# A gate over twelve consecutive tokens, the conv folded into the key-value product, and key products moved to GpSimd

## The chip, the cores and the metric

The kernel runs on one core of a Trainium2 chip. The metric is the device time of one execution in microseconds (us): the median of 3 runs of the kernel before is 76.44 us (75.55 to 77.24). The profiled execution took 76.63 us; the trace of it spans 74.9 us, so the measured time is about 1.7 us longer than the span of the trace.

Five engines work side by side: TensorE (PE in the profile; its weight loads are PEld), VectorE (DVE), ScalarE (ACT), GpSimd (POOL) and SyncE (SP, which here only issues transfers). Each works through its own instructions in order.

## The reference

Two layers, one after the other. The first is a linear attention with a second-degree feature map, the second a causal depthwise convolution that gates a linear unit. There are 4 batches, 4 heads, 1088 tokens, 32 elements per head.

```python
def phi(x):                          # S1, S2: 8 x 32
    a = einsum('rd,bhsd->bhsr', S1, x)
    b = einsum('rd,bhsd->bhsr', S2, x)
    return einsum('bhsi,bhsj->bhsij', a, b).reshape(..., 64)

q_p, k_p = phi(q), phi(k)
kv  = einsum('bhsf,bhsd->bhfd', k_p, v)          # sum over all tokens of a batch
z   = sum(k_p, axis=2)
num = einsum('bhsf,bhfd->bhsd', q_p, kv)
den = einsum('bhsf,bhf->bhs', q_p, z)[..., None] + 1e-06
x   = num / den                                  # heads side by side: b, s, 128

xp = concatenate([zeros((B, 4, 128)), x], axis=1)
gate_pre = sum over k of conv_w[k] * xp[:, k:k + S, :]      # 5 taps
gate = 1 / (1 + exp(-gate_pre))
out  = (gate * (x @ w_val)) @ w_out
```

## The kernel before

A batch's 1088 tokens are 32 blocks `j` of 34 consecutive tokens `T`; the 34 `T` (padded to 36) are 3 *units* of 12, and a unit is 3 *chunks* of 128 columns, 4 `T` by 32 `j`. There are N = 12 units in all. A main loop of *steps* works on several units at once, each a few steps further on: the keys of unit i+1, the queries of unit i-2, the gate of unit i-6, the output of unit i-7.

For the keys: a 32x32 block transpose on DVE, the projections `abk` on PE (fp32), a copy to SBUF on ACT, the outer products (two chunks on DVE, one on POOL), and the sums `kv` and `z` on PE.

```python
def k_phi(i):
    ...
    outer(DVE, phik, ab[:, 0, :ND]..., ab_sb[:, 1], 0, ND * H)     # ND = 2 chunks of 3
    outer(POOL, phip, ab_sb[:, 0]..., ab_sb[:, 1], ND * H, H)      # the third chunk

def k_z(i):                       # z by matmul; each chunk's product with all three, 96 columns
    for t in range(NCK):
        PE.matmul(kv_ps[b][t * HR : (t + 1) * HR, R2:], lhsT=..., rhs=ab_sb[:, t * HR : (t + NCK) * HR], ...)
```

When the three units of a batch are summed, `kv` becomes weights. The value weights `kw` are `kv` times `w_val`; the gate weights `wg` are `kv`, transposed, times each of the five taps:

```python
def finish_c(b):                  # z times S2: the third part of rhsq
    PE.matmul(c_ps, lhsT=s2t, rhs=zm, ...); SCA.copy(out=rhsq[b][:, 2, :], in_=c_ps)
def finish_kvm(b):
    PE.transpose(kvm_ps, kvx, identf); SCA.copy(out=kvm, in_=kvm_ps)
def finish_wg(b, g):              # twice per batch
    POOL.tensor_mul(wg[b][:, g], kvm[:, g]..., cwrep[:, :, ...])   # cwrep: conv_w, one copy per partition
```

For the queries: transpose, projections with `z` folded in, normalise, outer product, transpose back into feature-major columns `phiT`.

```python
def q_ab(i):
    ...  # 12 fp32 matmuls abq<-rhsq,qT
    SCA.copy(out=ac, in_=ab[:, 0:3:2]...)
    POOL.tensor_mul(prod[:, :, 0:r], ac[:, 0], ac[:, 1])
def q_den(i):
    DVE.reduce_sum(den, prod); DVE.reciprocal(rden, den)
    POOL.tensor_mul(an, ac[:, 0], rden...)
def q_phi(i):
    DVE.tensor_mul(phiq, an..., ab[:, 1]...)          # 768 elements per partition
def q_pt(i):
    ...  # 6 PE transposes of phiq into pt
    for g in range(2):
        SCA.copy(out=phiT[b][:, g, HALO:]..., in_=pt[:, g]...)
    if u == U - 1:
        ...  # halo: two POOL copies of the last 4 T of all blocks, one block further
```

A block's first tokens need the last four `T` of the block in front of it for the convolution. That is the *halo*; since those `T` lie in the third unit, the gate of a batch's first unit waits for its third unit here.

The gate and the output:

```python
def g_mm(i):     # 10 matmuls (5 taps, 2 halves) of 384 columns, then 2 for the value
    ...
    SCA.activation(out=gate, in_=g_ps, func=ACT.Sigmoid)
def g_gv(i):     DVE.tensor_mul(gv, gate, v_ps)
def g_out(i):
    ...          # 3 matmuls o_ps<-w_out_sb,gv, 1 or 2 ACT copies to o_sb
    for m in range(M4):      # 4 transfers per unit, runs of one token (512 bytes)
        (SCA if i == N - 1 and m % 2 else nc.sync).dma_start(out=o_d[:, T0 + m : last : M4, :], in_=o_sb[J * m : J * (m + 1), :nc_, :])
```

Loads are all issued by SP at the start: k and v of batch 0, q of batch 0, then k, v and q of each later batch, with `cwrep` (conv_w copied to 128 partitions, 320 KB) in batch 1. PSUM: three shared buffers for `abk` and `abq`, three for gate, value and output, one each for `kv` and `pt`.

Of the kernel before, what the change touches and what calls it, by code (L numbers as in the profile page):

```python
# [16 lines left out]
def kernel(  # L17
# [19 lines left out]

    nc = tc.nc
# [3 lines left out]
    P = 128  # L42
# [7 lines left out]
    HALO = (KT - 1) * J  # L50
    eps = 1e-6

    const = ctx.enter_context(tc.tile_pool(name="const", bufs=1))
    work = ctx.enter_context(tc.tile_pool(name="work", bufs=3))
    ps_ab = ctx.enter_context(tc.tile_pool(name="ps_ab", bufs=3, space=bass.MemoryType.PSUM))
# [14 lines left out]
    PE, DVE, SCA, POOL = (Pinned(e) for e in (nc.tensor, nc.vector, nc.scalar, nc.gpsimd))  # L70
# [10 lines left out]
    phiT = [ctile([P, 2, HALO + U * W], BF16, f"phiT{b}") for b in range(B)]  # L81
# [7 lines left out]
    cwrep = ctile([P, KT, P], F32, "cwrep")  # L89
    warm = ctile([P, 1], F32, "warm")  # L90

    def kq_rows(src, b):
        return src[b].rearrange("h (j T) d -> (h j) (T d)", j=J)

    def load_all(src, dst, b):
        nc.sync.dma_start(out=dst[:, : NT * D], in_=kq_rows(src, b))

    def load_v(b):
        for h in range(H):
            head = v[b, h]  # L100
            dst = v_sb[b][:, h].rearrange("p T d -> p (T d)")

            def rows(j0, j1, m0, m1, n):
                nc.sync.dma_start(  # L104
                    out=dst[M4 * j0 + m0 : M4 * (j1 - 1) + m1, : n * D],
                    in_=bass.AP(
                        tensor=head.tensor, offset=head.offset + (NT * j0 + TM * m0) * D,
                        ap=[[NT * D, j1 - j0], [TM * D, m1 - m0], [1, n * D]],
                    ),
                )  # L110

            if b < B - 1 or h < H - 1:
                rows(0, J, 0, M4, TM)
            else:
                rows(0, J - 1, 0, M4, TM)
                rows(J - 1, J, 0, M4 - 1, TM)
                rows(J - 1, J, M4 - 1, M4, NT - TM * (M4 - 1))

    DVE.memset(v_sb[B - 1][3 * J :, H - 1, NT - 3 * TM :, :], 0.0)
    load_all(k, k_sb[0], 0)  # L120
    for x, Sx in enumerate((S1, S2)):
        SCA.dma_start(out=s_raw[x * r : (x + 1) * r], in_=Sx)
    load_v(0)
# [4 lines left out]
    for _ in range(7):  # L128
        PE.matmul(warm_ps, lhsT=zeros[:, :P], rhs=zeros, start=True, stop=True)

    DVE.memset(warm, 0.0)
# [8 lines left out]
    )  # L140
    hm = ctile([P, H], F32, "hm")
    DVE.memset(hm, 0.0)
    for h in range(H):
        DVE.memset(hm[h * D : (h + 1) * D, h : h + 1], 1.0)
    S3 = ctile([P, 2, HR], F32, "S3")

    def fill_k(b):
        POOL.memset(k_sb[b][:, NT * D :], 0.0)

    def fill_q(b):  # L150
        POOL.memset(q_sb[b][:, NT * D :], 0.0)
        POOL.memset(phiT[b][:, :, :HALO], 0.0)
        POOL.tensor_copy(out=rhsq[b][:, 0:2, :], in_=S3)

    fill_k(0)
# [6 lines left out]
    for _ in range(2):  # L162
        PE.matmul(warm_ps, lhsT=zeros[:, :P], rhs=zeros, start=True, stop=True)
# [7 lines left out]

    m2 = ctile([P, 2], F32, "m2")
# [9 lines left out]
    def early_constants():  # L182
        POOL.memset(mz4, 1.0)
        for sign, base in ((1, 0), (-1, r - 1)):
            POOL.affine_select(
                out=mz4, in_=mz4, pattern=[[-sign * D, H], [-sign * r, H]],
                compare_op=ALU.is_ge, fill=0.0, base=base, channel_multiplier=sign,
            )
        for h in range(H):
            POOL.memset(m2[h * D : (h + 1) * D, h % 2 : h % 2 + 1], 1.0)  # L190
            POOL.memset(m2[h * D : (h + 1) * D, 1 - h % 2 : 2 - h % 2], 0.0)
        for i in range(NPROD):
            POOL.memset(prods[i][:, :, r:], eps)

    def late_constants():
        DVE.reduce_sum(mz, mz4.rearrange("p x h -> p h x"), axis=AX.X)
        POOL.tensor_copy(out=s2x, in_=S3[:, 1].unsqueeze(1).to_broadcast([P, NCK, HR]))
        s2_ps = ps_g.tile([NCK * HR, P], F32, tag="g", name="s2_ps")
        PE.transpose(s2_ps, s2x.rearrange("p t x -> p (t x)"), identf)
        SCA.copy(out=s2t, in_=s2_ps)  # L200
        POOL.tensor_copy(out=identity, in_=identf)

    def load_weights():
        POOL.memset(w_val_sb, 0.0)
        for g in range(2):
            gs = slice(R2 * g, R2 * (g + 1))
            POOL.dma_start(out=w_val_sb[gs, g], in_=moe_w_val[gs])
        POOL.dma_start(out=w_out_sb, in_=moe_w_out)


    load_all(q, q_sb[0], 0)
    for b in range(1, B):
        load_all(k, k_sb[b], b)
        load_v(b)
        if b == 1:
            nc.sync.dma_start(out=cwrep, in_=moe_conv_w.unsqueeze(0).to_broadcast([P, KT, P]))
        load_all(q, q_sb[b], b)
# [4 lines left out]
    zab = {}  # L222
    abks, abss, phks, abqs, acs, prs, ans, pqs, vgs, gvs = ({} for _ in range(10))
# [5 lines left out]
    def block_transpose(src, dst, u, order):  # L229
        DVE.transpose(  # L230
            out=dst[:, u * W : (u + 1) * W].rearrange(f"p (t {order}) -> p t m j", t=NCK, m=M4),
            in_=src.rearrange("p (m u t d) -> p u t m d", m=M4, u=U, t=NCK)[:, u],
        )


    def k_T(i):
        b, u = divmod(i, U)
        block_transpose(k_sb[b], kT[b], u, "j m")

    def k_ab(i):  # L240
        b, u = divmod(i, U)
        ab = ps_ab.tile([P, 2, NCK, HR], F32, tag="ab", name="abk")
# [6 lines left out]
        ab_sb = work.tile([P, 2, NCK * HR], F32, tag="ab_sb", name="ab_sb")  # L249
        SCA.copy(out=ab_sb, in_=ab.rearrange("p x t c -> p x (t c)"))  # L250
        abks[i], abss[i] = ab, ab_sb
        zab[i] = ab_sb

    ND = NCK - 1

    def k_phi(i):
        ab, ab_sb = abks.pop(i), abss.pop(i)

        def outer(eng, dst, a, bb, lo, n):
            eng.tensor_mul(  # L260
                dst,
                a.unsqueeze(3).to_broadcast([P, n, r, r]),
                bb.rearrange("p (x j) -> p x j", j=r)[:, lo : lo + n]
                .unsqueeze(2)
                .to_broadcast([P, n, r, r]),
            )

        phik = work.tile([P, ND * H, r, r], F32, tag="phik", name="phik")
        phip = work.tile([P, H, r, r], F32, tag="phip", name="phip")
        outer(DVE, phik, ab[:, 0, :ND].rearrange("p t (h i) -> p (t h) i", h=H), ab_sb[:, 1], 0, ND * H)  # L270
        outer(
            POOL, phip, ab_sb[:, 0].rearrange("p (x i) -> p x i", i=r)[:, ND * H :], ab_sb[:, 1],
            ND * H, H,
        )
        phks[i] = phik, phip

    def k_kv(i):
        b, u = divmod(i, U)
        phik, phip = phks.pop(i)
        for t in range(NCK):  # L280
            for h in range(H):
                src = phik[:, t * H + h] if t < ND else phip[:, h]
# [4 lines left out]
                    start=(h == H - 1 and u == 0 and t == 0),  # L287
                    stop=(u == U - 1 and t == NCK - 1),
# [289 lines left out]
```

## Time and profile before

| what | before |
|---|---|
| time, median of 3 | 76.44 us |
| span of the profiled run | 74.9 us |
| PE busy, weight loads busy | 53.8 us, 37.2 us |
| DVE, ACT, POOL busy | 46.4, 33.9, 31.6 us |
| HBM read, written | 7.28 MB, 2.23 MB |
| share of the last chain: PE, DVE, DMA | 37%, 17%, 12% |

Busy times overlap, so none of them is a bound by itself. The kernel has stages: loads run at 308 to 399 GB/s until about 20 us, the main loop fills the middle, and after the last unit's products only PE, ACT and the output transfers are at work. In the views a line `L68` stands for the helper that issues nearly all instructions, so rows are told apart by the tiles: `phiq<-an,abq` is the product that writes `phiq`. A name without a number (`kT`) stands for all buffers of that name. Tile names such as `mz` and `S` are those of the kernel with their digits cut.

A useful clock for the loop is the start of the twelve `phiq` products on DVE, one per unit: 19.36, 22.94, 26.55, 30.63, 34.64, 38.29, 42.69, 46.35, 50.87, 55.32, 57.70 and 60.74 us.

### The profile page before, as it was taken

How to read it: one execution, taken by the hardware profiler on the slowest of the kernel's cores; microseconds unless marked ns; L12 is line 12 of the kernel's file. 1: busy time of each engine (PE TensorE's matmuls, PEld its weight loads, DVE VectorE, ACT ScalarE, POOL GpSimd, SP SyncE). 2: the span in 40 equal slices, each digit the busy share in tenths (PEclk: the TensorE clock that was granted, in tenths of full speed). 3: DMA queues.
4: the chain of work that ended last, by engine and by line, in shares of the span. 5: the costliest groups of instructions: out<-in, count | busy, mean ns of one | idle time of the engine just before them, and what ended most of it. 6: DMA issues, size and time to landing. Idle time of an engine off the chain costs nothing.

```text
span 74.9 us, 2969 instructions
## 1 busy us (share of the span) xinstructions
PE 53.8 (72%) x1215; PEld 37.2 (50%) x1215; DVE 46.4 (62%) x104; ACT 33.9 (45%) x95; POOL 31.6 (42%) x94
## 2 busy tenths in 40 slices
PE   2969950969667549979679992997996995995000
PEld 0313930859445427666566852864744664652000
DVE  3019965093797889797999699769089482232000
ACT  0700410123162626383825845566658687366100
POOL 5400698402426595617474654195262663000000
PEclk9999997555999999999999999999999999999755
DMA  0898899999965600000022040121313123332540
GB/s 5 281 305 132 308 363 371 368 339 372 399 219 143 227 24 27 0 0 17 0 53 61 0 113 5 41 55 27 79 26 79 25 58 86 103 85 67 142 112 18
DMA packets 9058, 9.62 MB, mean 128 GB/s; under 512 B 1493, under 2 KB 7893, under 8 KB 9045
## 3 DMA queue, kind: packets, MB, share of 16 engines
q1 hardware_dynamic: 8517, 9.29, 39.3%
q0 software_dynamic: 304, 0.07, 0.9%
q8 instruction: 9, 0.15, 0.8%
q10 hardware_dynamic: 224, 0.08, 0.4%
q14 instruction: 4, 0.03, 0.1%
HBM read 7.28 MB, written 2.23 MB: 127 GB/s over the span
## 4 chain that ended last, share of the span: by engine, by line
PE 37%; DVE 17%; DMA 12%; ACT 7%; SPq 6%; POOL 6%; issue 6%; ACTq 0%; POOLq 0%
PE g_ps L68 11%; DMA k_sb<-in_k_dram 10%; PE abq L68 7%; PE v_ps L68 4%; ACT phiT L68 4%; DVE kT L68 4%; DVE phiq L68 4%; PE kv L68 4%; DVE gv L68 3%; SPq L104 3%; PE abk L68 3%; PE pt L68 3%; PE o_ps L68 3%; DVE phik L68 2%; DMA out_dram<-o_sb 2%
## 5 line engine op out<-in xcount | busy, mean ns | idle before, releaser
L68 PE MATMUL g_ps<-phiT,wg 128*64 128x384 bf16 (+1 forms) x120 | 12.3, 321 | 1.0 <-POOL phiT L68 0.8
L68 DVE TENSOR_TENSOR phiq<-an,abq 128x768 bf16<-128x768 f32 x12 | 11.4, 951 | 2.6 <-POOL an L68 2.3
L68 PE MATMUL abk<-S,kT 128*32 128x64 f32 x288 | 7.8, 260 | 5.3 <-DVE kT L68 4.5
L68 ACT COPY phiT<-pt 128x384 bf16<-128x384 bf16 x24 | 10.3, 482 | 2.8 <-PE pt L68 2.6
L68 DVE STREAM_TRANSPOSE kT<-k_sb 128x384 f32<-128x384 f32 x12 | 10.0, 859 | 0.8 <-DMA k_sb<-in_k_dram 0.8
L68 POOL TENSOR_TENSOR phip<-ab_sb 128x256 f32<-128x256 f32 x12 | 7.5, 628 | 6.3 <-ACT ab_sb L68 6.3
L68 PE MATMUL abq<-rhsq,qT 128*32 128x96 f32 x288 | 9.3, 260 | 1.2 <-POOL rhsq L68 0.8
L68 PEld LDWEIGHTS abk<-S,kT 128*32 128x32 f32 x288 | 6.0, 133 | 7.7 <-DVE kT L68 3.8
L68 POOL TENSOR_TENSOR prod<-ac 128x96 f32<-128x96 f32 x12 | 4.7, 390 | 11.5 <-ACT ac L68 11.5
L68 DVE TENSOR_TENSOR gv<-gate,v_ps 128x384 bf16<-128x384 bf16 (+1 forms) x12 | 6.0, 502 | 4.8 <-PE o_ps L68 2.5
L68 POOL TENSOR_TENSOR an<-ac,rden 128x96 f32<-128x96 f32 x12 | 4.2, 352 | 10.5 <-DVE rden L68 8.3
L68 ACT COPY ab_sb<-abk 128x192 f32<-128x192 f32 x12 | 3.9, 323 | 10.4 <-PE abk L68 9.6
L68 PEld LDWEIGHTS <-wg 128*64 128x64 bf16 x120 | 6.6, 109 | 3.8 <-issue 1.3
L68 DVE TENSOR_TENSOR phik<-abk,ab_sb 128x512 f32<-128x512 f32 x12 | 8.2, 684 | 0.4 <-ACT ab_sb L68 0.4
L68 ACT ACTIVATE gate<-g_ps 128x384 bf16<-128x384 f32 (+1 forms) x12 | 5.7, 476 | 5.4 <-PE g_ps L68 5.3
L68 PE MATMUL kv<-phik,v_sb 128*32 128x64 f32 x192 | 7.5, 237 | 0.5 <-issue 0.5
L68 PEld LDWEIGHTS abq<-rhsq,qT 128*32 128x32 f32 x288 | 6.8, 116 | 2.1 <-POOL rhsq L68 0.9
L68 ACT COPY ac<-abq 128x192 f32<-128x192 f32 x12 | 3.9, 322 | 8.1 <-PE abq L68 7.3
L68 POOL TENSOR_TENSOR wg<-kvm,cwrep 128x320 bf16<-128x320 f32 x8 | 6.9, 866 | 0.3 <-ACT kvm L68 0.3
L68 DVE STREAM_TRANSPOSE qT<-q_sb 128x384 f32<-128x384 f32 x12 | 6.6, 549 | 0.6 <-DMA q_sb<-in_q_dram 0.6
L68 ACT COPY o_sb<-o_ps 128x384 f32<-128x384 f32 (+2 forms) x16 | 6.1, 404 | 1.9 <-PE o_ps L68 1.6
L68 PE MATMUL pt<-identity,phiq 128*128 128x128 bf16 x72 | 6.1, 220 | 0.7 <-DVE phiq L68 0.7
(60 smaller groups left out, 77.5 us busy)
## 6 DMA issues: line engine op xcount, KB each, us to landing
k_sb<-in_k_dram SPq DMA_DIRECT2D x4, 544.0 KB, 7.9
q_sb<-in_q_dram SPq DMA_DIRECT2D x4, 544.0 KB, 7.1
v_sb<-in_v_dram SPq DMA_DIRECT2D x15, 144.0 KB, 5.2
out_dram<-o_sb SPq DMA_DIRECT2D x39, 48.0 KB, 1.6
cwrep<-in_moe_conv_w_dram SPq DMA_DIRECT2D x1, 320.0 KB, 6.9
out_dram<-o_sb SPq DMA_DIRECT2D x7, 32.0 KB, 1.6
v_sb<-in_v_dram SPq DMA_DIRECT2D x1, 139.5 KB
out_dram<-o_sb ACTq DMA_DIRECT2D x1, 48.0 KB, 1.6
```

The lines of the kernel that those rows point to most:

```text
L68: return lambda *a, **k: tc.keep_in_program_order(call(*a, **k))
L104: nc.sync.dma_start(out=dst[M4 * j0 + m0 : M4 * (j1 - 1) + m1, : n * D], in_=bass.AP(tensor=head.tensor, offset=head.offset + (NT * j0 + T ...
```

## The change

The change rewrites where the work stands; the arithmetic is that of the reference as before. Its purposes: take work off DVE, start the loop earlier, let a batch's first gate not wait for its third unit, and store the output in fewer and longer runs.

- **Keys.** After the first three units all three chunks' outer products are made on POOL (`ND = 0`). The first three units still give DVE two chunks.
- **Queries.** A chunk now holds four `T` by 32 `j` token-major, so the transpose of q is a plain one over 384 contiguous columns, and `phiT` is written by one ACT copy of 768 elements. The units of a batch are taken in the order 2, 0, 1, so that the halo is ready first. The halo is one POOL copy.
- **Gate.** 12 consecutive `T`; `g_gv` writes its product reordered, so that an output partition holds three consecutive tokens: runs of 1.5 KB, one transfer per unit (two for a batch's last unit).
- **Conv weights.** `wg` no longer comes from a transpose and two POOL products: two fp32 matmuls multiply `kv` with a constant `dcw` (a diagonal per tap), and ACT copies them to bf16. `cwrep` goes; conv_w is loaded as 5 rows.
- **z** is 3 matmuls of 32 columns, `c` is 4 small matmuls.
- **Loads.** k and q of batches 2 and 3 are issued by POOL within the loop; the others by SP, in another order. The constants are set up earlier on POOL.
- **PSUM.** `abk` has one buffer of its own, shared with `c`, `kw` and half of `wg`; `abq` has two.
- The whole step has a new order.

```diff
-    ps_ab = ctx.enter_context(tc.tile_pool(name="ps_ab", bufs=3, space=bass.MemoryType.PSUM))
+    ps_k = ctx.enter_context(tc.tile_pool(name="ps_k", bufs=1, space=bass.MemoryType.PSUM))
+    ps_q = ctx.enter_context(tc.tile_pool(name="ps_q", bufs=2, space=bass.MemoryType.PSUM))
 ...
+    SP.dma_start(out=s_raw[:r], in_=S1)
+    SCA.dma_start(out=s_raw[r:], in_=S2)
+    load(k, k_sb, 0)
+    SCA.dma_start(out=cw_nat, in_=moe_conv_w)
+    load(q, q_sb, 0)
+    load(k, k_sb, 1)
     load_v(0)
+    load_v(1)
+    load(q, q_sb, 1)
+    load_v(2)
+    load_v(3)
 ...
+    def n_dve(i):
+        return 2 if i < U else ND                  # ND = 0
 ...
+    def finish_wg(b):
+        for g, (pool, tag) in enumerate(((ps_k, "k"), (ps_g, "g"))):
+            wg_ps = pool.tile([P, KT, 2 * D], F32, tag=tag, name="wg_ps")
+            PE.matmul(wg_ps, lhsT=fin["kvx"][gs], rhs=dcw[gs], start=True, stop=True)
+        for g in range(2):
+            SCA.copy(out=wg[b][:, g], in_=wps[g])
-        POOL.tensor_mul(wg[b][:, g], fin["kvm"][:, g]..., cwrep[:, :, ...])
 ...
+    QU = (2, 0, 1)
 ...
+            if i < N - 1:
+                SP.dma_start(out=rows, in_=src)
+            else:
+                for m in range(nm):
+                    (SCA if m % 2 else SP).dma_start(out=rows[m], in_=src[J * m : J * (m + 1)])
 ...
+    k_T(0); k_ab(0); k_cp(0); constants_1(); k_T(1); k_ab(1); k_cp(1); k_z(0); constants_2()
+    k_T(2); k_ab(2); k_cp(2); k_phiP(0, 2); k_z(1); q_T(0); k_z(2); k_phiD(0); finish_zm(0)
+    finish_c(0); k_phiP(1, 2); k_phiP(2, 2); k_phiD(1)
+    for s in range(2, N + 3):
+        ...                                         # at s == 2 also q_ab(0), k_T(3), q_T(1), k_phiD(2), load k of batch 2
+        k_ab(s + 1); k_cp(s + 1); q_ab(s - 2); q_cp(s - 2)
+        q_phi(s - 3); g_gv(s - 6); q_prod(s - 2); k_kv(s)
+        q_den(s - 2); k_phiP(s + 1, 2); q_an(s - 2); k_T(s + 2); q_T(s)
+        k_phiP(s + 1, 1); k_phiP(s + 1, 0)
+        q_pt(s - 3); q_ev(s - 3); q_halo(s - 3); g_val(s - 5)
+        g_out(s - 6); g_ev(s - 6); g_st(s - 6)
+        ...                                         # finish_kw, finish_wg, finish_c, finish_kv by step
+        g_mm(s - 5); g_sig(s - 5)
+        ...                                         # s == 2, 3, 4: load q2, k3, q3 on POOL
+    # after the loop: value, gate and output of the last two units
```

(Shortened: the calls of a step are written without their range checks, and setup code is left out.)

## The prediction

> **What bounds the kernel now.** I read the busy line first, then busy time by stage, one step of the loop on DVE and on PE, the costs of the POOL operations, and last the transfers at the end.
>
> ```profile
> PE 53.8 (72%) x1215; PEld 37.2 (50%) x1215; DVE 46.4 (62%) x104; ACT 33.9 (45%) x95; POOL 31.6 (42%) x94
> ```
>
> 72% for PE is an average over stages. The stage table (start:end, length, busy PE, PEld, DVE, ACT, POOL, granted clock, DMA share, GB/s) says more:
>
> ```profile
> 15.00:23.00 8.00, 5.49 (x150) 4.81 (x151) 5.78 (x14) 2.97 (x10) 2.26 (x7) 0.74 0.92 316
> 23.00:34.00 11.00, 8.41 (x293) 6.49 (x296) 9.88 (x21) 5.81 (x17) 6.33 (x16) 1.00 0.20 68
> 34.00:51.00 17.00, 14.21 (x379) 10.18 (x367) 14.48 (x32) 9.85 (x29) 10.03 (x24) 1.00 0.15 38
> 51.00:62.00 11.00, 10.16 (x156) 6.50 (x157) 7.43 (x16) 7.54 (x22) 4.99 (x14) 1.00 0.20 52
> 62.00:70.00 8.00, 5.64 (x56) 3.39 (x53) 2.08 (x4) 4.71 (x13) 0.58 (x2) 1.00 0.33 87
> ```
>
> To 23 us loads run (DMA 0.92) and nothing is full; from 23 to 51 DVE is busy 24.4 of 28 us and PE 22.6; later DVE drops out. One step in the timeline of DVE (start, length):
>
> ```profile
> 34.64 0.95 DVE L68 TENSOR_TENSOR phiq<-an,abq 128x768 bf16<-128x768 f32 x1 [0.48 <-POOL an L68]
> 35.51 0.68 DVE L68 TENSOR_TENSOR phik<-abk,ab_sb 128x512 f32<-128x512 f32 x1
> 36.11 0.85 DVE L68 STREAM_TRANSPOSE kT<-k_sb 128x384 f32<-128x384 f32 x1
> 36.81 0.54 DVE L68 STREAM_TRANSPOSE qT<-q_sb 128x384 f32<-128x384 f32 x1
> 37.27 0.22 DVE L68 TENSOR_REDUCE den<-prod 128x12 f32<-128x108 f32 x1
> 37.53 0.23 DVE L68 RECIPROCAL rden<-den 128x12 f32<-128x12 f32 x1
> 37.67 0.49 DVE L68 TENSOR_TENSOR gv<-gate,v_ps 128x384 bf16<-128x384 bf16 x1
> 38.13 0.19 DVE L68 TENSOR_TENSOR zm<-kv,mz 96x32 f32<-96x32 f32 x1
> 38.29 0.95 DVE L68 TENSOR_TENSOR phiq<-an,abq 128x768 bf16<-128x768 f32 x1
> ```
>
> Each starts where the last one leaves off: this step is 3.65 us of DVE with no gap. By start-to-start it is phiq 0.87, phik 0.60, kT 0.70, qT 0.46, den 0.26, rden 0.14, gv 0.46, zm 0.16. Between the phiq of 19.36 and of 50.87 us lie 8 steps, so a step takes 3.94 us: DVE's 3.65 or less plus a wait. PE is close behind:
>
> ```profile
> 46.66 0.54 PE L68 MATMUL abk<-S,kT 128*32 128x64 f32 x24
> ...
> 48.12 1.00 PE L68 MATMUL g_ps<-phiT,wg 128*64 128x384 bf16 x10
> 49.05 0.50 PE L68 MATMUL v_ps<-phiT,kw 128*128 128x384 bf16 x2
> 49.39 0.50 PE L68 MATMUL pt<-identity,phiq 128*128 128x128 bf16 x6
> 49.72 0.33 PE L68 MATMUL o_ps<-w_out_sb,gv 128*128 128x128 bf16 x3
> 49.98 0.28 PE L68 MATMUL kv<-ab_sb 128*32 128x96 f32 x3
> ```
>
> From 46.66 to 49.98 PE passes a whole step in 3.3 us: abk, z, kv and abq 1.46, gate 0.93, value 0.34, pt 0.33, out 0.26. POOL in the groups (busy, mean ns):
>
> ```profile
> L68 POOL TENSOR_TENSOR phip<-ab_sb 128x256 f32<-128x256 f32 x12 | 7.5, 628 | 6.3 <-ACT ab_sb L68 6.3
> ...
> L68 POOL DMA_DIRECT2D w_val_sb<-in_moe_w_val_dram x2 | 1.2, 610 | 0.3 <-POOL w_val_sb L68 0.3
> ```
>
> One chunk's product costs POOL 0.63 us where two cost DVE 0.68; a small transfer costs its issuer 0.61. The end, on SP's queue:
>
> ```profile
> 55.03 17.66 SPq L484 DMA_DIRECT2D out_dram<-o_sb  x30
> ```
>
> The last result is in SBUF at 69.58, but SP issues until 72.69: some 0.45 us per transfer with four per unit, a backlog. 1.6 us later (median landing) the last one lands; the span ends at 74.9.
>
> **What the Trainium skill says.** "GPSIMD Engine Reference", section 4.1 (Engine selection), puts two-input elementwise work on GpSimd at about half of VectorE's speed. The trace agrees for this form: 2.45 ns per element against 1.34. "FP8 and Floating Point Precision", section "TensorE Precision Notes", counts four passes through the array for true fp32; no row shows passes, and the trace has two matmul records per fp32 call (24 for 12). I use it for `wg`. "DMA: Bandwidth & Descriptors", section "Issuing engines are not separate DMA queues", says another issuing engine saves only the sequencer's time. The backlog above is just that time, so longer runs with fewer issues should show.
>
> **Part by part, in four stages.**
>
> *Start to the first phiq (19.36 now).* S1 and S2 come by two queues, an estimated 0.4 us sooner, so kT(0) starts near 5.4 (now 5.84). But DVE's second instruction is the reduction to `mz`, which waits for POOL, where the constants now stand first: memsets and mask 1.2, three weight transfers 1.8, identity 0.3, some ten small memsets 1.4, `id64` 0.3, `dcw` about 0.8 (320 elements at 2.45 ns), `mz4` 0.6 — from 0.8 to about 7.4 us, by the rows of before. So kT(1) starts near 7.6, later than now. Then kT(2), qT(0), phik(0) end near 10.2. abk(2) needs the PSUM buffer phik(0) reads, so it follows: +0.5 abk, 0.35 copy, 0.3 z, 0.2 zm, 0.4 c, 0.2 copy, and abq(0) runs near 12.3 to 13.0. Now it runs at 16.3, since a whole later unit and its load (k at 12.11) stood in front. DVE from zm on: phik 0.6, kT 0.7, qT 0.46, phik 0.6, den and rden 0.5, kT 0.7, qT 0.46, kvx 0.2, in all 4.2. First phiq near 16.3: 3.1 us gained.
>
> *Eleven steps to the last phiq (41.4 now, to 60.74).* DVE loses phik: 3.65 - 0.60 = 3.05, no bound any more. POOL has three phip at 0.66, prod 0.36, an 0.36: 2.7 per step, plus a halo of about 0.3 in three; the two wg (0.83 each) and the fills go. In the steps s = 2, 3, 4 it also issues a transfer of 544 KB, estimated at 0.8, and den waits behind that: I walked these to phiq at 16.3, 19.2, 23.0 and 26.5, two of the three near 3.6. PE: z is narrower (-0.05) and c and the transpose go (-0.35 per batch), while wg adds 320 columns x 4 passes / 2.4 per ns = 0.53 us per matmul by the skill's passes, 0.53 to 1.07 per batch. So 3.3 + 0.3 = 3.55 to 3.6 per full step: **PE becomes the bound**. ACT: ab_sb 0.32, ac 0.32, phiT about 0.8, o_sb 0.5, gate 0.5, plus a third of kvt, kw, wg and rhsq (1.8): 3.0. Five full steps at 3.65 make 18.25; the next has no abk (3.3), the last two neither abk nor kv (2.6 each). Sum 10.2 + 18.25 + 8.5 = 36.95, last phiq at 53.25: 4.4 us gained.
>
> *Last phiq to the last o_sb (8.84 now).* With the units in the order 2, 0, 1 the gate of the batch's first unit needs no halo of the last: the POOL copy (0.30) and the 0.82 us PE waits for it go. From phiq: 1.0 to pt, then PE 4.4 (pt 0.33, three values 1.0, gates 0.93 + 0.93 + 0.8, two outputs 0.4), gate 0.45, gv 0.5, output 0.5, copy 0.53, with small gaps 7.5: 1.3 gained, o_sb at 60.75.
>
> *Last o_sb to the end (5.3 now).* No backlog: one transfer for each earlier unit. The last unit's six go three on SP and three on ACT, 3 x 0.43 + 1.6 + 0.6 = 3.5: 1.8 gained.
>
> Span 64.2. The measured time lies 1.7 above the profiled span: 65.9. I add 0.6 for waits a sum of busy times leaves out: **66.5 us**.
>
> **Rivals.** (1) *POOL becomes the bound.* phip has no slack in the early steps, and a 544 KB transfer may cost the issuer more than 0.6 us. For it: prod, an and den form a loop through POOL, DVE and back. Against: 2.7 per step is under PE's 3.55. If POOL needed 3.7 per step, the time would be some 69. (2) *PSUM turns into waits.* abk has one buffer, shared with c, kw and wg; PE would wait for ACT once or more per step. At 0.4 per step it gives back 4 us: 70. (3) *Loads.* k2, q2, k3 and q3 start at about 12 us or later, beside v; if q1 or k2 comes late, early steps slip by up to 2 us: 68. The 544 KB transfers land in 7 to 8 us now, and k2 is wanted near 22, so I don't expect it. (4) *Better than thought:* wg's two matmuls use different rows of the array and may overlap, and PE may reach 3.4: 64.
>
> **Range and chances.** The stages gain 3.1, 4.4, 1.3 and 1.8; the last two rest on plain rows, the first two on walks that can be off by 2 us each, mostly to the slow side: 62.8 to 71. To lose the whole gain, two rivals would have to hold in full: faster 0.93, within 2% 0.04, slower 0.03.
>
> **What would show it right or wrong.** First phiq at 16 to 17 us; steps of 3.5 to 3.8 between the phiq of units 3 and 8 with PE over 90% busy there and DVE under 85%; no SP backlog and under 4 us after the last o_sb; no PE wait for the POOL halo. Wrong, if den, an or kv wait on POOL in late steps (rival 1), abk on ACT (2), or kT or qT on a load (3).

## The result and the profile after

The changed kernel takes 73.12 us (median, 72.50 to 73.63), the kernel before on the same chip 76.38 us. The ratio is 0.958 with a 95% interval of 0.945 to 0.971. On another chip, in a later set, the ratio was 0.971 (0.962 to 0.981). So the change makes the kernel faster by 3 to 4%, where 13% was predicted: the direction was right, the size was not, and 73.1 lies above the predicted range. (In most sets some runs were a few per cent longer than the rest; the ratios leave them out, the medians don't.)

The busy line of the kernel after, which answers to the first line shown of before:

```profile
PE 52.3 (73%) x1250; PEld 37.0 (52%) x1250; DVE 41.3 (58%) x107; ACT 35.6 (50%) x92; POOL 35.6 (50%) x94
```

DVE lost 5.1 us of work and POOL gained 4.0, as the change meant. The span fell only from 74.9 to 71.6 us. The stage table, in the same stretches as before (start:end, length, busy PE, PEld, DVE, ACT, POOL, granted clock, DMA share, GB/s):

```profile
15.00:23.00 8.00, 6.02 (x223) 4.75 (x211) 6.08 (x14) 4.08 (x10) 7.26 (x16) 1.00 0.70 231
23.00:34.00 11.00, 10.37 (x299) 7.72 (x299) 8.57 (x20) 7.30 (x18) 8.12 (x18) 1.00 0.27 87
34.00:51.00 17.00, 15.59 (x426) 11.81 (x424) 13.00 (x32) 11.85 (x32) 9.79 (x21) 1.00 0.19 52
51.00:62.00 11.00, 9.32 (x112) 5.67 (x111) 4.84 (x11) 6.89 (x17) 1.42 (x4) 1.00 0.22 63
62.00:70.00 8.00, 0.56 (x5) 0.22 (x3) 0.55 (x2) 1.25 (x4) 0.00 (x0) 0.63 0.34 70
```

From 23 to 51 us PE is now busy 26.0 of 28 us and DVE 21.6: the two have changed places. The last row is the surprise. From 62 us on almost nothing computes, yet the kernel runs for nearly 10 us more. Before, that stretch still held 5.64 us of PE.

The clock of the twelve `phiq` on DVE now reads 16.15, 19.39, 23.08, 27.00, 30.24, 34.34, 38.55, 41.75, 45.27, 49.05, 51.87 and 55.48 us; the last `o_sb` is written at 63.94. With these the span splits as the prediction split it:

| stage | before | predicted | after |
|---|---|---|---|
| start to first phiq | 19.36 | 16.3 | 16.15 |
| first to last phiq | 41.4 | 36.95 | 39.33 |
| last phiq to last o_sb | 8.84 | 7.5 | 8.46 |
| last o_sb to the end | 5.3 | 3.5 | 7.66 |
| span | 74.9 | 64.2 | 71.6 |

The last stage was to become shorter by 1.8 us and became longer by 2.4.

A step on DVE and the start of one on PE (start, length; in brackets the idle time before it and what ended it):

```profile
34.34 0.91 DVE L70 TENSOR_TENSOR phiq<-an,abq 128x768 bf16<-128x768 f32 x1
35.18 0.54 DVE L70 TENSOR_TENSOR gv<-gate,v_ps 128x256 bf16<-128x256 bf16 x2
36.79 0.27 DVE L70 TENSOR_REDUCE den<-prod 128x12 f32<-128x108 f32 x1 [1.07 <-POOL prod L70]
```
```profile
34.79 0.54 PE L70 MATMUL abk<-S,kT 128*32 128x64 f32 x24 [0.30 <-ACT rhsq L70]
35.15 0.68 PE L70 MATMUL abq<-rhsq,qT 128*32 128x96 f32 x24
```

DVE now has a hole of 1.07 us in a step that had none. PE has almost none; the one shown is a wait of 0.30 us for ACT. POOL makes all later `phip`, 30 in place of 12, each as long as before:

```profile
L70 POOL TENSOR_TENSOR phip<-ab_sb 128x256 f32<-128x256 f32 x30 | 18.4, 625 | 3.0 <-ACT ab_sb L70 3.0
L70 POOL TENSOR_TENSOR prod<-ac 128x96 f32<-128x96 f32 x12 | 4.6, 386 | 13.0 <-ACT ac L70 9.8 <-PE kv L70 3.2
```

POOL stands idle 13 us in front of `prod`, waiting for ACT and PE, so it is not the bound of the full steps. In the early steps it comes near to it: from 15 to 23 us it is busy 7.26 of 8 us, two issues of loads (0.59 us each) among that. The issues of output on SP, and the tail in stretches of 1 us, in the same columns as above:

```profile
29.78 36.30 SPq L70 DMA_DIRECT2D out_dram<-o_sb  x17
```
```profile
64.00:65.00 1.00, 0.00 (x0) 0.00 (x0) 0.00 (x0) 0.00 (x0) 0.00 (x0) 0.50 0.25 95
65.00:66.00 1.00, 0.00 (x0) 0.00 (x0) 0.00 (x0) 0.00 (x0) 0.00 (x0) 0.50 0.41 64
66.00:67.00 1.00, 0.00 (x0) 0.00 (x0) 0.00 (x0) 0.00 (x0) 0.00 (x0) 0.50 0.84 127
67.00:68.00 1.00, 0.00 (x0) 0.00 (x0) 0.00 (x0) 0.00 (x0) 0.00 (x0) 0.50 0.59 118
68.00:69.00 1.00, 0.00 (x0) 0.00 (x0) 0.00 (x0) 0.00 (x0) 0.00 (x0) 0.50 0.14 51
69.00:70.00 1.00, 0.00 (x0) 0.00 (x0) 0.00 (x0) 0.00 (x0) 0.00 (x0) 0.50 0.05 15
```

SP has 17 issues for the whole output where the kernel before has 46, and it issues the store of unit 10 at 62.75 us, as soon as that result is in SBUF. So the backlog of issues is indeed gone. Instead the transfers themselves are slow: while a unit is stored the 16 DMA engines are busy 0.25 on average and move some 95 GB/s. A share of 0.25 is what 4 engines of 16 would give. The new store has the pattern `m j (c e)` in DRAM, and its outermost dimension `m` has four entries.

The Trainium skill states this rule: "DMA: Bandwidth & Descriptors", section "Why a DMA increments its semaphore by 16 and not by 1", says that a transfer is spread over the largest number of engines, up to 16, that divides the size of the slowest dimension of both its patterns. Here the two sizes are 4 (`m`) and 128 (the partitions of `o_sb`), which gives 4, and the measured share of 0.25 agrees. The prediction cited that page for the cost of issuing and passed over this rule.

**Theory after the result.** (A) Most of the miss is the tail: stores on four engines, with the last unit's pieces behind the store of the unit before. (B) The drain adds to it: near the end PE waits for the last `phiq` (1.18 us) and for PSUM buffers. Rivals: (C) the tail is the issue and landing of the last unit's own six transfers; (D) DVE or POOL still sets the steps, and moving the outer products was worth little; (E) the shared PSUM buffer `ps_k` costs the steps.

### The profile page after: what moved, and what is told of

Read it like the earlier page. It is cut to its first block, busy times and chain, and to the rows that moved or that the text cites. A ratio compares the mean times of both kernels' runs of the same rounds, so it can differ in the third digit from the quotient of the medians.

```text
span 71.6 us, 2999 instructions
## 1 busy us (share of the span) xinstructions
PE 52.3 (73%) x1250; PEld 37.0 (52%) x1250; DVE 41.3 (58%) x107; ACT 35.6 (50%) x92; POOL 35.6 (50%) x94
## 4 chain that ended last, share of the span: by engine, by line
PE 41%; POOL 17%; DVE 12%; issue 10%; ACT 8%; POOLq 1%; ACTq 0%
PE abq L70 8%; PE abk L70 8%; PE g_ps L70 7%; PE kv L70 6%; POOL phip L70 5%; DVE kT L70 5%; POOL prod L70 4%; PE pt L70 3%; PE wg_ps L70 3%; ACT gate L70 3%; DVE phiq L70 3%; PE v_ps L70 2%; POOL w_val_sb L70 2%; DVE den L70 2%; PE o_ps L70 2%
## 5 line engine op out<-in xcount | busy, mean ns | idle before, releaser
L70 POOL TENSOR_TENSOR phip<-ab_sb 128x256 f32<-128x256 f32 x30 | 18.4, 625 | 3.0 <-ACT ab_sb L70 3.0
L70 ACT COPY phiT<-pt 128x768 bf16<-128x768 bf16 x12 | 9.6, 798 | 5.3 <-PE pt L70 5.3
L70 PE MATMUL g_ps<-phiT,wg 128*64 128x384 bf16 (+1 forms) x120 | 11.6, 320 | 0.3 <-ACT gate L70 0.2
L70 DVE TENSOR_TENSOR gv<-gate,v_ps 128x384 bf16<-128x384 bf16 (+2 forms) x16 | 6.6, 431 | 5.5 <-ACT gate L70 5.5
L70 PEld LDWEIGHTS <-wg 128*64 128x64 bf16 x120 | 7.1, 109 | 3.5 <-issue 2.7
L70 DVE TENSOR_REDUCE den<-prod 128x12 f32<-128x108 f32 x12 | 3.2, 266 | 6.7 <-POOL prod L70 6.7
L70 PE MATMUL kv<-phip,v_sb 128*32 128x64 f32 x240 | 6.1, 229 | 0.0
L70 PE MATMUL v_ps<-phiT,kw 128*128 128x384 bf16 (+1 forms) x24 | 5.7, 317 | 0.3 <-ACT gate L70 0.3
```

The source lines that it names most:

```text
L70: return lambda *a, **k: tc.keep_in_program_order(call(*a, **k))
```

## The experiments

The kernels below are the changed kernel with the edit shown, unless another base is named. "Tail" is from the end of the last `o_sb` to the end of the span.

| run | what | time, us (n) | ratio to before | tail, us |
|---|---|---|---|---|
| e1_jm | all units' stores with j outermost | 70.63 (4) | | 3.4 |
| e2_split | four transfers per unit | 71.22 (4) | 0.932 (0.922 to 0.942) | 5.6 |
| e3_two | two transfers per unit, m of 2 outermost | 80.22 (1) | | 9.85 |
| e7_jmtail | j outermost in the last two units only | 70.25 (4) | 0.927 (0.915 to 0.940) | 3.8 |
| e13_skip10 | store of unit 10 left out | 69.65 (6) | 0.918 (0.909 to 0.927) | 3.8 |
| e14_after | the changed kernel, beside e13, e15, e16 | 73.68 (6) | 0.971 (0.962 to 0.981) | 7.5 |
| e15_jmtail | e7 again, beside them | 69.85 (6) | 0.926 (0.920 to 0.932) | 3.8 |
| e4_nd2 | two of three key chunks on DVE | 79.94 (4) | 1.053 (1.042 to 1.063) | |
| e5_nd2_sbuf | the same, DVE reads SBUF | 76.62 (4) | 1.011 (1.002 to 1.021) | |
| e6_qu | units in the order 0, 1, 2 | 80.25 (4) | 1.042 (1.028 to 1.056) | |
| e8_tail_all | e7 + last abq earlier + free PSUM | 69.38 (4) | 0.913 (0.903 to 0.923) | 4.1 |
| e16_tail_all | e8 again | 69.65 (6) | 0.913 (0.903 to 0.924) | 3.9 |
| e9_wgbf | e7 + bf16 wg | 70.82 (4) | 0.928 (0.913 to 0.943) | |
| e10_kwpt | e7 + kw_ps in pt's buffer | 70.90 (4) | 0.943 (0.930 to 0.956) | |
| e12_pedose | e7 + more matmuls in each gate | 71.71 (4) | 0.956 (0.943 to 0.969) | |
| e11_all | e8 + e9 + e10 | 70.23 (4) | 0.922 (0.906 to 0.937) | |

### The tail: how many engines store

**e1_jm.** `gv` is written so that an output partition's row is `(j, m)`, and the store has the 32 `j` outermost; the last unit goes in two transfers.

```diff
-    gv[:, lo:hi].rearrange("p (c m j) -> p m c j", ...)
+    gv[:, lo:hi].rearrange("p (c j m) -> p m c j", ...)
-    rows = o_d[...].rearrange("j (m c) e -> m j (c e)", m=nm)     # m = 4 outermost
+    rows = o_d[...].rearrange("j (m c) e -> j m (c e)", m=nm)     # j = 32 outermost
```

> The changed kernel with only the output's order altered: the gate product is written so that an output partition is j times 4 plus m, and each unit is stored with j (32) as the slowest dimension instead of m (4); the last unit goes as two transfers (one on SP, one on ACT) instead of six. Theory A (a store whose slowest dimension is 4 runs on 4 of the 16 DMA engines, and the last two units' stores queue there): while stores run the rate rises from about 97 GB/s, and the 7.7 us between the last o_sb and the end shrink to about 3 us, so the time falls by 4 to 5 us, to about 68.5 us. Rival B (the end is long because the last unit's six transfers are issued on two queues): it shrinks too, so this run alone does not part A and B. Rival C (the end is fixed work after the last transfer, or larger stores simply take long): no change, 73 us. The products gv may get a little slower by the new write order; over 0.1 us each would show on DVE.

The tail fell from 7.66 to 3.4 us, and the first full stretch of a store moved twice as much:

```profile
65.00:66.00 1.00, 0.00 (x0) 0.00 (x0) 0.00 (x0) 0.53 (x2) 0.00 (x0) 1.00 0.52 197
```

But `gv` now writes single bf16 elements four apart and takes twice as long (the group's row ends in busy us, mean ns, and idle time):

```profile
L70 DVE TENSOR_TENSOR gv<-gate,v_ps 128x384 bf16<-128x384 bf16 x8 | 8.2, 1019 | 4.0 <-ACT gate L70 4.0
```

In the changed kernel the same row has a mean of 549 ns. From the fourth `phiq`, behind which the first `gv` stands, to the last one it is 28.93 us here and 28.48 there, and from there to the last `o_sb` 8.77 against 8.46: 0.8 us is given back on DVE. (The last `phiq` comes 1.3 us later, at 56.81, but the larger part of that lies in front of the first `gv`.) The four times run from 68.75 to 71.34 us, and no ratio is on record.

**e2_split.** Each unit is stored as before by block of `j`, four transfers of 48 KB, each with `j` outermost.

```diff
-    if i < N - 1: SP.dma_start(out=rows, in_=src)
-    else:
-        for m in range(nm): (SCA if m % 2 else SP).dma_start(out=rows[m], ...)
+    for m in range(nm): (SCA if i == N - 1 and m % 2 else SP).dma_start(out=rows[m], ...)
```

> The changed kernel with each unit's store split into one transfer per m (4 issues of 32 partitions, 48 KB each) in place of one of 192 KB; order of data, the last unit's six transfers and everything else are kept. Theory A (4 of 16 engines): each transfer now has 32 as its slowest dimension and spreads over all engines; 7.7 us after the last o_sb become about 4.2 us (SP's backlog of issues comes back for the second last unit, 4 x 0.45 us), time about 69.5 us. Rival B (the last six issues): they are unchanged and more issues stand in front of them, so the end gets no shorter, 73 us or more. Rival C: 73 us.

The tail is 5.6 us: between the two. The stores reach a DMA share of 0.68 and 173 GB/s (65 to 66 us), but SP has 53 issues and is busy with them until 67.57 us, 3.2 us after the last result. This is the backlog of the kernel before.

**e3_two**, the dose in the other direction: two transfers per unit, each with two entries in `m`.

```diff
-    SP.dma_start(out=rows, in_=src)
+    for m in range(0, nm, 2):
+        SP.dma_start(out=rows[m : m + 2], in_=src[J * m : J * (m + 2)])
```

> The dose: each unit's store in two transfers with a slowest dimension of 2 (64 partitions, 96 KB each). Theory A: each runs on 2 engines; if both use the same two, the rate while storing halves from 97 to about 50 GB/s, a unit's store takes about 4 us, longer than a step, and the end comes 5 us or more later than in the changed kernel (span 76 us or more); if they use different engines, the span stays near 71.6. Rivals B and C: span 71 to 72, rate while storing unchanged.

```profile
64.00:65.00 1.00, 0.00 (x0) 0.00 (x0) 0.00 (x0) 0.46 (x1) 0.00 (x0) 1.00 0.14 49
65.00:66.00 1.00, 0.00 (x0) 0.00 (x0) 0.00 (x0) 0.02 (x1) 0.00 (x0) 1.00 0.13 47
```
```profile
ACT o_sb L70 <- DMA out_dram<-o_sb: 4.9, 2, 3.0
```

Share and rate are halved: 0.13 to 0.14 and 47 to 49 GB/s for two entries, against 0.25 and 95 GB/s for four. The two transfers of a unit do not add up to the share of one with four entries. At that rate the stores no longer keep up with the end of the loop, and the wait list shows ACT waiting 4.9 us for an `o_sb` buffer. The time, 80.22 us, is that of a single execution. Rate and share follow the outermost dimension; this is shown in both directions.

**e7_jmtail.** The cheap cure: the new order for the last two units only, so that the other ten keep the fast `gv`.

```diff
+    order = "j (m c) e -> j m (c e)" if i >= N - 2 else "j (m c) e -> m j (c e)"
```

> The store of 16 engines (j slowest) and the j-m order of gv for the last two units only; the other units keep the cheap write order and the store on 4 engines. Theory A says the 4-engine stores hurt only where nothing follows them: the end after the last o_sb is about 3.4 us as with the order used everywhere, and the middle is as in the changed kernel (gv 0.55, not 1.02 us), so 69 us, lower than both runs that altered all units (70.6 and 71.2 us). If the 4-engine stores also slow the middle, it is no faster than those.

70.25 us, tail 3.8. From the fourth `phiq` to the last it is 28.50 us, as in the changed kernel (28.48). So the loop pays nothing. The two slower `gv` cost 0.3 us in the drain (8.76 us from the last `phiq` to the last `o_sb`, against 8.46), and the whole gain is in the tail.

**e13_skip10, e14_after, e15_jmtail**, on one chip. In e13 the store of unit 10 is left out: that part of the output stays unwritten, the last unit is stored as in the changed kernel.

```diff
-    if i < N - 1: SP.dma_start(out=rows, in_=src)
+    if i < N - 2: SP.dma_start(out=rows, in_=src)
+    elif i == N - 2: pass
```

> The changed kernel without the store of unit 10 (its 192 KB of the output are left unwritten); all else as it is, the last unit's six transfers too. Theory A (the tail is the wait of the last unit's pieces behind unit 10's store, which runs on four engines): last o_sb to the end falls from 7.66 us to 4-5 us and the time from 73.1 to 70-70.8 us, as much as with the store of both units on all engines. Rival B (the last unit's own six transfers, their issue and their landing are what takes long): the tail stays at 6.5 us or more, the time at 72 us or more.

> The changed kernel itself, beside the next two on one chip, so that the sizes of the two steps below can be read against it: 73.1 us.

> The stores of the last two units on all engines, nothing else, beside the changed kernel on the same chip. If the store's few engines are the main part of the miss: 2.5-3.5 us less than the changed kernel (69.6-70.6 us).

The tail of e13, to be held against that of the changed kernel above:

```profile
64.00:65.00 1.00, 0.00 (x0) 0.00 (x0) 0.00 (x0) 0.00 (x0) 0.00 (x0) 0.50 0.55 168
65.00:66.00 1.00, 0.00 (x0) 0.00 (x0) 0.00 (x0) 0.00 (x0) 0.00 (x0) 0.50 0.24 64
66.00:67.00 1.00, 0.00 (x0) 0.00 (x0) 0.00 (x0) 0.00 (x0) 0.00 (x0) 0.50 0.00 0
```

The store with 32 entries outermost, in e15:

```profile
64.00:65.00 1.00, 0.00 (x0) 0.00 (x0) 0.00 (x0) 0.40 (x2) 0.00 (x0) 0.50 0.67 249
```

With unit 10's store away, the last unit's six transfers are through by 66 us. With it, they are not through before 69. By the ratios, the time falls by 4.0 us (0.971 to 0.918), and with both units stored with `j` outermost by 3.4 (0.926). The intervals of these two ratios, 0.909 to 0.927 and 0.920 to 0.932, overlap and both lie far from the 0.962 to 0.981 of the changed kernel. Rival C is out: the last unit's own transfers need 3.8 us, near the 3.5 predicted. The rest was the queue behind unit 10's store.

### The steps: what the moved products are worth

**e4_nd2.** `ND = 2`: DVE makes two of three key chunks, as in the kernel before.

> One part of the change undone: DVE makes two of three chunks' key products in all units (as before the change), POOL one. If PE is the bound of the full steps and DVE's relief made that so: DVE needs 3.65 us per step again against PE's 3.55 to 3.65, the five intervals between phiq of units 3 and 8 grow from 18.3 to about 20 us and the time by 1 to 3 us, to 74 to 76 us. Rival (POOL's three products are what holds kv and the loop up): POOL falls to 1.4 us per step, prod and an come sooner, and the time falls by 1 us or more.

79.94 us: 6.8 above the changed kernel, and more than expected. The five full intervals of `phiq` take 22.06 us, in place of 18.27. DVE is busy 17.60 us of them, no more than 80%, so its load is not all of it. The timeline of PE shows the other part:

```profile
46.19 0.81 PE L70 MATMUL wg_ps<-dcw,kvx 64*128 64x320 f32 x4 [0.75 <-DVE phik L70]
```

`phik` reads `abk` in PSUM, and with the new allocation `abk`, `wg_ps`, `kw_ps` and `c_ps` share one buffer: PE waits until DVE has read it. The five full intervals have four such waits, 3.0 us in all.

**e5_nd2_sbuf.** The same, but from the fourth unit on DVE takes both factors from the copy in SBUF.

```diff
-    outer(DVE, phik, abk[i][:, 0, :n]..., bb, n * H)
+    outer(DVE, phik, abs_[i][:, 0]... if i >= U else abk[i][:, 0, :n]..., bb, n * H)
```

> Two chunks of the key products on DVE in all units, as in the run before this one that took 79.9 us, but from the fourth unit on DVE reads both factors from ab_sb in SBUF instead of one from the PSUM buffer of abk. Theory D (that run lost its 7 us mostly because DVE's late phik held the single PSUM buffer that abk, c, kw and wg share, so PE stood still): most of the loss comes back, to 74 to 76 us, and the 0.76 us waits of PE on phik are gone; what remains over 73.1 is DVE's load of 3.65 us per step. Rival (DVE's load itself, or phik delaying kT, is the loss): it stays at 79 us or more.

```profile
43.96 0.27 DVE L70 TENSOR_REDUCE den<-prod 128x12 f32<-128x108 f32 x1 [0.24 <-POOL prod L70]
```

76.62 us. So of the 6.8 us, 3.3 were the PSUM buffer held by DVE, and 3.5 are left for the work on DVE itself. In the five full intervals DVE is busy 17.63 of 19.38 us, with one hole of 0.24 to 0.48 us in each. Moving the products to POOL is thus worth some 3.5 us, and the part of rival D that concerns DVE is out. But only 1.1 us of it lies in these full steps (19.38 against 18.27 us). Most of the rest is in the three intervals before them: 13.31 us here, 10.85 in the changed kernel. The move also has a hidden second use: with a reader on DVE, the single buffer of `abk` costs 3.3 us.

**e6_qu.** `QU = (0, 1, 2)`: the units of q in their natural order, so that the gate of a batch's first unit waits for the halo of its third again.

> The changed kernel with the query units of a batch in the order 0, 1, 2 instead of 2, 0, 1, so that the halo again comes from the last unit. If the order is worth what I think: in one step of each batch PE waits for pt, the phiT copy (0.80 us) and the halo copy (0.39 us) before the gate, with only 0.5 us of its own work to fill it, 0.7 us per batch, so the time grows by 2 to 3 us to 75 or 76, with PE waits on POOL phiT in the list. Rival (hidden by PE running behind): within 0.5 us of 73.1.

80.25 us, far more than expected. The wait list names the cause (total us, times, longest):

```profile
PE g_ps L70 <- POOL phiT L70: 4.8, 4, 2.1
```

One wait per batch, of 0.7 to 2.1 us. The profiled execution took 86.47 us, so I take no more from it than this new wait. The two shortest times, 78.69 and 79.19, lie 5.8 us above 73.1; the four waits are 4.8 of that at most, and what makes up the rest is not shown. In the kernel before, the trace has this wait in the last batch alone (0.82 us).

**e12_pedose.** On e7: in the gates of units 0 to 6 the first tap is multiplied three times (the first two results are overwritten), four matmuls of 384 columns more per step (320 in a batch's third unit).

```diff
-    for kk in range(KT):
+    for kk in ((0, 0) if i < 7 else ()) + tuple(range(KT)):
```

> Built on the same version (70.25 us). In the gates of units 0 to 6 the first tap is multiplied three times instead of once (the first two are overwritten by the third): four more matmuls of 384 columns, some 0.37 us of PE in each of seven steps, nothing else. Theory A (PE is the bound of the full steps, idle 0.2-0.3 us at most in each): the five full steps each grow by 0.25-0.37 us and the time by 1.5-2.6 us: 71.8-72.8 us. Rival B (a loop through ACT, POOL and DVE sets the step and PE has room): under 0.8 us, 70.3-71.0 us.

The dose and the period of a batch, read from one `wg_ps` to the next on PE:

```profile
30.27 0.81 PE L70 MATMUL wg_ps<-dcw,kvx 64*128 64x320 f32 x4
31.11 1.33 PE L70 MATMUL g_ps<-phiT,wg 128*64 128x384 bf16 x14
...
42.31 0.81 PE L70 MATMUL wg_ps<-dcw,kvx 64*128 64x320 f32 x4
```

The same two in e15:

```profile
29.12 0.81 PE L70 MATMUL wg_ps<-dcw,kvx 64*128 64x320 f32 x4
...
40.66 0.81 PE L70 MATMUL wg_ps<-dcw,kvx 64*128 64x320 f32 x4
```

The period is 12.04 us; in e15 it is 11.54. The three gates of a batch are 0.33, 0.27 and 0.32 us longer, 0.92 in all, and the period grows by 0.50, about half of it. The waits of PE on ACT for `kw` and on `kT` (0.20 and 0.18 us in e15) are gone and took most of the rest. The five full intervals take 19.08 us in place of 18.27: 0.81 more, where theory A wanted 1.25 to 1.85. The time rose by 1.5 us by the medians and by 2.2 by the ratios, as theory A had it, but a part of that lies in the early intervals, which differ from run to run. So PE is nearly the bound, but not alone.

**e9_wgbf**, the dose with the other sign, on e7: the products for the gate weights in bf16.

```diff
-    dcw = ctile([P, KT, 2 * D], F32, "dcw")       ... lhsT=fin["kvx"][gs]
+    dcw = ctile([P, KT, 2 * D], BF16, "dcw")      ... lhsT=fin["kvt"][gs]
```

> Built on the version with the stores of the last two units on all engines (70.25 us). The gate weights' products are made from the bf16 kv and a bf16 diagonal instead of two fp32 operands; everything else stays. Theory A (PE sets the pace in the full steps, and fp32 costs it several passes): the two wg_ps matmuls of a batch fall from 0.74-0.81 us to about 0.3 us, so each of the steps with wg in the PE-bound stretch (two of the four batches; the first stands before the kT wait, the last before the drain's own wait) is 0.45-0.5 us shorter: 69.2-69.6 us. Rival B (the wg steps are set by ACT's or POOL's chain): the records get shorter, the intervals between the phiq do not: 70.0-70.4 us.

```profile
31.22 0.31 PE L70 MATMUL wg_ps<-dcw,kvt 64*128 64x320 bf16 x2
32.06 1.00 PE L70 MATMUL g_ps<-phiT,wg 128*64 128x384 bf16 x10 [0.53 <-ACT o_sb L70]
```

The two bf16 matmuls one by one (duration in ns: least, median, most):

```profile
L70 PE MATMUL wg_ps<-dcw,kvt x8: 306/306/307, 18.3 to 53.3; 64*128 64x320 bf16 x8
```

`wg_ps` takes 0.31 us in place of 0.81, as theory A said, and the gate behind it starts not a bit sooner: from the start of `wg_ps` to the gate it is 0.84 us here and 0.85 in the changed kernel. The new wait of 0.53 us for ACT, which has to empty a PSUM buffer, takes the exact place of what PE saved. The period stays at 11.56 us and the ratio at 0.928 (e7: 0.927). Rival B of this run is right. Each matmul takes 0.306 us and both together 0.31: they run side by side.

**e10_kwpt**, on e7: `kw_ps` leaves the shared buffer.

```diff
-    kw_ps = ps_k.tile([P, 2, P], F32, tag="k", name="kw_ps")
+    kw_ps = ps_pt.tile([P, 2, P], F32, tag="pt", name="kw_ps")
```

> Built on the same version (70.25 us). kw_ps moves from the single PSUM buffer that it shares with abk, c_ps and wg_ps into the one of pt, so c_ps needn't wait for the copy of kw. Theory A (the shared buffer is a cost on the path): the waits of c_ps for ACT's kw, 1.05 us in the first batch and 0.20 us in two later ones, go, and some of the 0.30 us waits behind them: 0.5-1.5 us less, 68.8-69.8 us. Rival B (c_ps is followed by rhsq on ACT and by abk waiting for kT, which end no earlier): another wait takes its place and the time stays at 70.0-70.4 us.

```profile
PE kw_ps L70 <- ACT phiT L70: 1.8, 3, 0.9
```

`c_ps` no longer waits for `kw`, but `kw_ps` waits for ACT to empty `pt`, 0.9 us in the first batch and 0.45 in the next two. The period grows to 12.00 us, and 70.9 us is no gain. Of rival E it can be said that the shared buffer costs some waits, but they can't be had back by a move to another buffer that ACT empties later still.

### The drain

**e8_tail_all.** On e7: the last `abq`, its copy and `prod` a step earlier; `den` and `an` of the last unit before `gv`; the last gates and values in PSUM buffers of pools that stand empty by then.

```diff
+    if s == N: q_ab(N - 1)                     # was in step N + 1; then q_cp, q_prod
+    if s == N + 1: q_den(N - 1); q_an(N - 1)   # ahead of g_gv
-    g_ps = ps_g.tile(...)
+    g_ps = (ps_q if i == N - 1 else ps_g).tile(...)
-    v_ps = ps_g.tile(...)
+    v_ps = (ps_q if i == N - 1 else ps_k if i == N - 2 else ps_g).tile(...)
```

> That kernel, and two changes in the drain: the last unit's abq, its copy and prod are issued one step earlier, before the gate of unit 7, and its den and an before gv; and the last two units' value and gate use the PSUM buffers that are free by then. Theory E (the drain is set by the chain abq, ac, prod, den, rden, an, phiq, pt of 3.0 us, which PE's work of 2.9 us no longer covers, and by PSUM buffers): the 1.18 us wait of PE before the last pt goes, and some 0.75 us of PSUM waits after it, so the time falls 1.5 to 2 us below the run without them, to about 67.3 us. Rival (PE's work bounds the drain too): within 0.5 us of it.

> The same, with the last abq hoisted by a step and the last gates and values in free PSUM buffers. Theory A (the 1.18 us for which PE waits for the last phiq, and the PSUM waits after it, are on the path): 0.6-1.5 us less than the kernel with the new stores alone. Rival B (PE finds other waits there): within 0.3 us of it.

In the changed kernel the last transposes stand so on PE:

```profile
56.49 0.51 PE L70 MATMUL pt<-identity,phiq 128*128 128x128 bf16 x6 [1.18 <-DVE phiq L70]
```

and in e8 so:

```profile
54.82 0.34 PE L70 MATMUL o_ps<-w_out_sb,gv 128*128 128x128 bf16 x3 [0.47 <-DVE gv L70]
...
56.00 0.51 PE L70 MATMUL pt<-identity,phiq 128*128 128x128 bf16 x6
...
57.12 0.46 PE L70 MATMUL o_ps<-w_out_sb,gv 128*128 128x128 bf16 x3 [0.28 <-DVE gv L70]
```

The wait of 1.18 us is gone, and so are the two for ACT after it; the output products now wait for `gv` (0.47, 0.28 and 0.29 us more). From the ninth `phiq` to the last `o_sb` it is 18.07 us in e8, 18.99 in e7: 0.9 us gained in the trace, where theory E wanted 1.5 to 2. In e16 and e15 it is 18.08 and 18.98. In time the two are not clearly apart: on one chip 69.65 against 69.85, and the intervals 0.903 to 0.924 and 0.920 to 0.932 overlap. The gain is shown in the traces; the times neither confirm nor exclude it.

**e11_all.** e8 with the edits of e9 and e10.

> The version with the stores of the last two units on all engines, the last abq hoisted by a step and the last gates and values in free PSUM buffers (69.38 us), with the bf16 wg and the kw_ps in pt's buffer added. Theory A: both savings add: 67.2-68.5 us. Rival B (each only gives its time to the next wait): 69.0-69.5 us.

Ratio 0.922 (0.906 to 0.937), the best runs at 69.01 and 69.18: no further gain. The lowest ratio is that of e8, 0.913 of the time of before (0.903 to 0.924 in both sets); the interval of e11 covers it.

## Why the prediction missed

**Last o_sb to the end: the step that failed.** It said "No backlog: one transfer for each earlier unit" and "3 x 0.43 + 1.6 + 0.6 = 3.5". The backlog of issues did go. But the step counted transfers as if their number alone mattered: 1.6 us of landing was that of the old 48 KB pieces, whose outermost dimension is 32. A 192 KB store with four entries outermost moves 95 GB/s, an estimate of 2 us for it alone, and the last unit waits behind it. Even the issues are held up: the last one on each of SP and ACT takes 1.4 us, in e13 no more than 0.43. Measured 7.66 instead of 3.5: 4.2 us of the 7.4 by which the span came out too long (6.6 in time). e13 and e15 give 4.0 and 3.4 us of it back, e3 shows the dose. With the queue free the step's sum holds (3.8).

**The last three steps, "3.3, 2.6 and 2.6".** They took 3.78, 2.82 and 3.61, together 1.7 us too many. The working summed PE's records and left out the waits. In the first of them PE waits 0.20 us for ACT's copy of `kw` and 0.30 for `rhsq`. In the last one PE, with no `abk` and `kv` left, runs out of cover for the chain `abq`, `ac`, `prod`, `den`, `an`, `phiq`: it waits 1.18 us for the last one. Hoisting it brings that interval to 2.63 and the last `o_sb` 0.9 us nearer.

**Last phiq to last o_sb, 7.5.** It took 8.46. The term "PE 4.4" was 5.4, from the start of `pt` to the last output product of unit 10: `g_ps` and `v_ps` wait for ACT's gate to empty a buffer (0.15 and 0.30 us), with gaps beside.

**Five full steps, 18.25.** They took 18.27, which is in part luck. By the working's own terms PE's step is 3.5 us (3.3, less 0.05, plus a third of what `wg` adds and `c` and the transpose save), not the 3.65 that was used. PE is indeed busy 3.50 us per step (17.52 of 18.27 us), and waits, which the sum has no term for, make the rest. "PE becomes the bound" holds only in part: 0.5 us less PE work per batch gained nothing (e9), and 0.92 us more cost 0.50 (e12). From these two I conclude that PE and the emptying of PSUM by ACT set the step together. The estimate of "0.53 to 1.07" for `wg`, worked out from the four passes of the Trainium skill's page "FP8 and Floating Point Precision", section "TensorE Precision Notes", contains the measured 0.81 us. Since the two matmuls run side by side (e9), 0.53 is the end to compare with, and it was too low by 0.28; no row shows the passes.

**Start and early steps.** The first `phiq` was predicted for 16.3 and came at 16.15. Some steps on the way were off and made up for each other: `kT(0)` starts at 5.77 and not at 5.4, since it waits for `k` and not for S; POOL's constants do not hold up `mz`, which starts at 6.75 and not at 7.4. No run takes this gain of 3.2 us apart. The next three intervals took 10.85 us against 10.2; in runs with the same early program they vary from 10.3 (e14) to 11.7 (e1), so this is within their scatter.

**The rivals.** The sign named for rival 1 did appear: `den` waits on POOL's `prod` in every step. But in the full steps POOL itself is then waiting for ACT's `ac` or for PE, so it does not set the pace. In the three early intervals rival 1 has a point: POOL stands idle only 1.5 of 10.85 us there, in e14 0.8 of 10.31. No DVE instruction waits for a load after 6 us, so loads were not late for DVE. The sign for rival 2 appeared too (`abk` waits 0.30 us for ACT, twice). PE's waits for ACT to empty or fill its buffers are 1.05 us once and 0.15 to 0.30 after that, in all 2.8 us, spread over the kernel, under the 4 us of that rival. Of rival 4 one half came true: the two `wg` matmuls overlap, but PE's busy time stays at 3.50 us per step. The rival that came true in full, a transfer made slower by its shape, was not among the four. The 0.6 us added for waits was too little: the two stages between the first `phiq` and the last `o_sb` took 3.3 us more than their sums. The 1.7 us above the span hardly differs from the 2.0 of the profiled execution (73.63 us).

## What to carry to other kernels

When a change makes transfers fewer and longer, read the outermost dimension of both their patterns before their number: here a rearrangement to `m j (c e)` brought a store down to a quarter of the DMA share and lengthened the end more than the saved issues shortened it (7.66 us, against 5.6 with three times the issues in e2). Give the last transfers, behind which nothing hides, the pattern with the most entries outermost, even at the price of a slower instruction before them, and leave the others as they are cheapest. When an engine is busy 96% of a loop, as PE is here, look also at who empties the buffers it writes to before taking work off it: 0.5 us saved on PE turned into 0.53 us of waiting for PSUM.

## What the runs showed beyond that

- Store rate by the outermost dimension: 2 entries 47 to 51 GB/s at a DMA share of 0.13 to 0.14; 4 entries 95 to 100 GB/s at 0.25 to 0.26; 32 entries up to 249 GB/s at 0.67 within 1 us (e15). From the first two, an estimate of some 24 GB/s per engine.
- A bf16 product on DVE of 384 elements per partition takes 549 ns when its output has runs of 32 elements, and 1019 ns when each element stands four from the next.
- Two fp32 matmuls with 320 columns and 64 rows take 0.81 us in four records, the same in bf16 0.31 us in two. The bf16 ones take 0.306 us each, so two matmuls on different rows of the array, into different PSUM buffers, run at the same time here.
- The order 2, 0, 1 of the units, which the prediction credited with 1.1 us in the drain, is worth some 5.8 us in the changed kernel: with the natural order PE waits 0.7 to 2.1 us for the halo in each of the four batches.
